# Weight decoding in a fused attention and squared-ReLU kernel: part of it moved to GpSimd, late weights two halves a piece, and three products held to the end

## The chip, the cores and the metric

The program runs on one NeuronCore of a Trainium2 chip. The metric is the device time of one execution in microseconds; for the kernel before the median of three runs is shown, and one execution was profiled.

## The reference, cut to what matters

```python
f = 1.0 / (1.0 + np.exp(-f_logit))              # B, H, S, D = 4, 8, 768, 48
for t in range(S):
    state = f[:, :, t, :, None] * state + np.einsum('bhd,bhe->bhde', k[:, :, t], v[:, :, t])
    y[:, :, t] = np.einsum('bhd,bhde->bhe', q[:, :, t], state)
x = y.transpose(0, 2, 1, 3).reshape(B * S, H * D)   # 3072 tokens x 384
h = x @ w_in                                        # 384 -> 2048
g = np.maximum(h, 0.0) ** 2
out = g @ w_out                                     # 2048 -> 384
```

A gated linear attention gives 3072 tokens of 384 numbers; two matrix products with a squared ReLU between them follow. The weights arrive as 64-bit floats.

## The kernel before, in words

**Tiling.** The 768 positions are cut into six blocks of 128; a block with its four batches is a tile of 512 columns. For every block the 2048 hidden units are taken in 16 *pieces* of 128. A piece `f` has three steps: `up` (L257, L277) makes `ph[f]` in PSUM from the block's `x` and the weights `w[f, 0]`; `square` (L283) and `rest` (L302) turn it into two f16 tiles, `gh` and `gl`, a high and a low part; `down` (L308) adds the products with `w[f, 1]` to three PSUM banks `po[0..2]`. Every product is made of three f16 matmuls (high by low, low by high, high by high), so `up` and `down` are nine 128x512 matmuls each. `ph` has two banks, three in the last block.

**Decoding a weight half.** A *half* is `w[f, i]`, 128x384 numbers, `i` = 0 for `w_in` and 1 for `w_out`. Its raw 64-bit words are loaded by a DMA from SP (`weights_load`, L453). `decode` (L141) then has four steps: ScalarE converts the upper 16 bits into `head` (L149); VectorE joins these with bits of the lower word into a float `wa` (L152); ScalarE makes the high f16 part (L162); VectorE makes the low part as a difference (L164). Four buffers of `head` and four of `wa` rotate.

**Attention units.** Each block has four *units*, a pair of heads each (the fourth collects left-over rows of the others). A unit has stages with one letter each (L708): gates `G` on ScalarE, `K` (two scans and products on VectorE, L503 and L511, and two small GpSimd operations, L507 and L510), `Q` (L517, L519, L522), `m` (DMAs that copy rows into `last_kq`, which the fourth unit reads; for units 0, 1, 4 and 5 they are issued by GpSimd, L530), `r` (ScalarE copies, L541), `D` and `S` (matmuls), `C` and `M` (VectorE), `Y` (matmuls), `H` and `X` (the halves of `x`), `g` and `h` (DMAs of the left-over rows, L704; `g` by GpSimd for the first two blocks).

**Order of the work.** All engines run in program order (`tc.manual_schedule`, L810). For blocks 0 and 1 that order is written out by hand in two strings, `FIRST` (L81) and `SECOND` (L86), one token a step. In them `A I c J` are the four decoding steps of `w[n, 0]`, `B O d P` those of `w[n, 1]`, `e n a w` those of a small fourth set of rows; `U`, `R`, `E`, `W` are `up`, `square`, `rest` and `down` of block 0. The strings decode the halves of pieces 0 to 7 and compute block 0's attention and pieces 0 to 7 and block 1's attention. After them come the runs of `order` (L822): block 1 with all 16 pieces, block 0 with pieces 8 to 15, then blocks 2 to 5. Steps are hung into a run with `hook(k, n, place, do)`: run `k`, piece `n`, place 0 (before `up`), 0.5 (after `square`), 0.7 (after `rest`) or 1 (at the piece's end). So the 16 halves of pieces 8 to 15 are decoded in the run of block 1, three in every two pieces, from piece 1 to piece 11 (L845 to L870); each is loaded four pieces ahead, behind a small VectorE memset that marks the time (L457). The units of later blocks are hung by `SLOTS` and `STAGE_AT`: for the first of them the gates and `K` fall at piece 6 of block 1, `Q` at piece 7, for the second `K` at piece 8, `Q` at piece 9.

**The end.** In a run `down` follows `up` by two pieces (`LAG`), in the last block by four (`LAST_LAG`). There the last four `down`s are done one `po` bank after the other (L325 to L334), each bank is scaled into `ob_last` (L332), and behind the first bank the *verdict* ends: the kernel checks that its numbers were in the range of f16 (`verdict`, L927) and reads a flag into a register on every engine (L905), on which a branch (L1092) depends that would compute everything another way. The outputs of the last block are written to DRAM behind that branch (L1098 to L1101). The first part of the verdict (four memsets, L937 to L940, two small copies, eight matmuls, L946 to L951, and reductions) hangs at the end of piece 7 of the last block (L901).

Of the kernel before, what the change touches and what calls it, by code (L numbers as in the profile page):

```python
# [12 lines left out]
F32 = mybir.dt.float32  # L13
# [10 lines left out]
P = 128  # L24
# [18 lines left out]
LARGE = 60000.0  # L43


X_SCALE, W_SCALE, G_SCALE = 2.0**16, 2.0**7, 2.0**18
ROOT = 2.0**-8
R_SCALE = G_SCALE**0.5 / (X_SCALE * W_SCALE)
O_SCALE = 1.0 / (G_SCALE * W_SCALE)
# [4 lines left out]
LAG = 2  # L54
LAST_LAG = 4
GBUF = 5
AHEAD = 4
LO = 8
SPLIT = 2
# [35 lines left out]
class Moe:  # L95


    def __init__(self, ctx, tc, const, sums, out):
        self.tc, self.nc, self.sums, self.out = tc, tc.nc, sums, out

        self.const, self.w, self.row, self.ps, self.turns, self.first = const, {}, {}, {}, 0, []
        self.xs, self.w4, self.third_bank, self.heads, self.half = [], None, None, 0, True

    def words(self, f, i):

# [32 lines left out]
    def upper(self, t, dt):  # L138
        return t.bitcast(dt).rearrange("p (n two) -> p n two", two=2)[:, :, 1]

    def decode(self, row, parts):  # L141


        nc = self.nc
        high, low = self.planes(row)
        rows, n = row.shape
        head = self.head[self.heads % HEADS][:rows, :n]
        self.heads += 1
        nc.scalar.copy(out=self.upper(head, F16), in_=high)  # L149
# [7 lines left out]
        yield from self.halves(parts(), a)  # L157

    def halves(self, w, a):
        nc = self.nc  # L160
        if self.half:
            nc.scalar.mul(out=w[:, 0], in_=a, mul=W_SCALE)  # L162
            yield
            nc.vector.scalar_tensor_tensor(  # L164
                out=w[:, 1], in0=a, scalar=W_SCALE, in1=w[:, 0], op0=ALU.mult, op1=ALU.subtract
            )
        else:
            nc.scalar.copy(out=w[:, 0], in_=a)
            yield
            nc.vector.tensor_tensor(out=w[:, 1], in0=a, in1=w[:, 0].bitcast(F32), op=ALU.subtract)  # L170
        yield

    def heads_in(self, pool):
# [109 lines left out]
    def square(self, f):  # L283

        nc, ph = self.nc, self.ph[f]
        dt = F16 if self.half else F32R
        gh, gl = (
            self.gp.tile([P, NT], dt, tag=t, name=f"{t}{self.blk}_{f}") for t in ("gh", "gl")
        )
        if self.half and f == 0:  # L290
            gh = self.pers.tile([P, NT], F16, name=f"first{self.blk}")
            self.first.append(gh)
        nc.scalar.activation(ph, ph, AF.Relu, scale=R_SCALE if self.half else 1.0)  # L293
        nc.scalar.activation(ph, ph, AF.Square)  # L294
        if self.half:
            n = 2 * NF + self.blk * NF + f
            nc.scalar.activation(gh, ph, AF.Copy, accum_out=self.sums[:, n : n + 1])  # L297
        else:
            nc.scalar.copy(out=gh, in_=ph)
        self.g[f] = gh, gl  # L300
# [17 lines left out]
    def run(self, hooks, obs=None, before=None, lag=LAG, ends=()):  # L318


        for n in range(len(self.fs) + lag):
            if before and not obs and n == len(self.fs) + lag - 1:
                return
            self.at = n
            if obs and n == len(self.fs):  # L325
                for e in range(NJ):
                    for f in self.fs[-lag:]:
                        self.down(f, (e,))
                    if e < len(ends):
                        ends[e]()  # L330
                    for _, cs in tails(e):
                        self.nc.vector.tensor_scalar(  # L332
                            out=obs[e][:, cs], in0=self.po[e][:, cs], scalar1=O_SCALE, scalar2=None, op0=ALU.mult
                        )  # L334
                return
            if n < len(self.fs):
                for hook in hooks.get((n, 0), ()):
                    hook()
                f = self.fs[n]
                self.up(f)  # L340
                self.square(f)
                for hook in hooks.get((n, 0.5), ()):
                    hook()
                self.rest(f)
                for hook in hooks.get((n, 0.7), ()):
                    hook()
            if before and n == 0:
                before()
                self.sums_of()
            if n >= lag:  # L350
                self.down(self.fs[n - lag])
            for hook in hooks.get((n, 1), ()):
                hook()
# [61 lines left out]
def fast_path(ctx, tc, moe, ident, low, fkqT, vN, w, w4, out):  # L415
# [338 lines left out]
    def step(t):  # L754
# [17 lines left out]
        elif nm == "j":  # L772
            nc.sync.dma_start(moe.fourth_words(), w4.bitcast(I16)[:, 1:])
        elif nm in "enaw":
            if nm == "e":
                decoding["fourth"] = moe.decode(moe.row4, moe.fourth_parts)
            next(decoding["fourth"])
        elif nm in "AIcJBOdP":
            i = "AIcJBOdP".index(nm) // 4
            if nm in "AB":  # L780
                decoding[n, i] = moe.decode(moe.row[n, i], lambda: moe.parts(n, i))
            next(decoding[n, i])
        elif nm in ("ua", "ub", "uc"):
# [26 lines left out]
    with tc.manual_schedule(engines={ET.PE, ET.SP, ET.DVE, ET.Activation, ET.Pool}):  # L810
# [14 lines left out]
        def hook(k, n, at, do):  # L825
            while n >= len(order[k][1]):
                k, n = k + 1, n - len(order[k][1])
            hooks[k].setdefault((max(n, 0), at), []).append(do)

        def third():  # L830
            early.close()
            moe.inputs(ctx)
            xs[2] = moe.new_x(2, 2)

# [2 lines left out]

        def advance(h):  # L840
            if h not in steps:
                steps[h] = moe.decode(moe.row[halves[h]], lambda: moe.parts(*halves[h]))
            next(steps[h], None)

        for n in range(1, NF - 1):  # L845
            few = range(3 * (n - 1) // 2, min(3 * n // 2, len(halves)))
            for h in few:
                if n < AHEAD:
                    weights_load(*halves[h])
                else:  # L850
                    hook(0, n - AHEAD, 0.5, lambda h=h: weights_load(*halves[h], mark=True))

            def before(few=few):
                for h, last in zip(few, (None, *few)):
                    for m in (h, h, last):
                        if m is not None:
                            advance(m)

            def after(few=few[:-1]):
                for h in few:  # L860
                    advance(h)

            def last(few=few):
                for h in few[-1:]:
                    advance(h)
                    advance(h)


            for place, do in zip((0, 0.5, 0.7) if n > 1 else (0.7, 0.7, 0.7), (before, after, last)):
                hook(0, n, place, do)  # L870
# [27 lines left out]
        for blk in range(NBLK):  # L898
            for j in range(NJ):
                hook(blk if blk > 1 else 1 - blk, TOP_AT + j, 1, lambda blk=blk, j=j: moe.size_of(blk, j, xs[blk][j]))  # L900
        hook(len(order) - 1, VERDICT_AT, 1, lambda: next(found))  # L901
        ends = (
            lambda: general.append(next(found)),
            lambda: None,
# [2 lines left out]
        for k, (blk, fs) in enumerate(order):  # L907
# [3 lines left out]
            if blk == NBLK - 1:  # L911

                moe.third_bank = ps_a
                obs = moe.third_of("ob_last")
                moe.run(hooks[k], obs, owed, LAST_LAG, ends)
                moe.third_bank = None
            else:
                moe.run(hooks[k], None, owed)
# [8 lines left out]
def verdict(nc, moe, low, ident, pool):  # L927
# [22 lines left out]
    nc.tensor.matmul(pt[0:1, 1, :DM], lhsT=sel[:, NBLK : NBLK + 1], rhs=v, start=True, stop=True)  # L950
    nc.tensor.matmul(  # L951
        pt[0:1, 1, DM : DM + 1], lhsT=tinies[:, 0:1], rhs=tinies[:, 1:2], start=True, stop=True
    )
    V.tensor_reduce(
        out=good[:, 0:1], in_=low.rearrange("p u n -> p (u n)"), axis=mybir.AxisListType.X, op=ALU.min
    )
    for n, x, least in (
        (1, pt[:NBLK, 0], ENOUGH), (2, pt[0:1, 1, :DM], ENOUGH), (3, pt[0:1, 1, DM : DM + 1], P * TINY**2 * 0.999)
# [19 lines left out]
def general_path(ctx, tc, moe, ident, fkqT, vN, w, out):  # L978

    nc = tc.nc  # L980
    moe.half = False
# [181 lines left out]
```

## Time and profile before

| | us |
|---|---|
| median of 3 runs | 468.21 (468.12 to 469.08) |
| the profiled execution's own time | 467.79 |
| its span in the trace | 466.1 |
| PE / PEld busy | 441.0 / 222.6 |
| DVE / ACT / POOL busy | 251.3 / 304.4 / 28.9 |

PE is TensorE's matmuls, PEld its weight loads, DVE VectorE, ACT ScalarE, POOL GpSimd, SP the engine that issues most DMAs. A busy time is the union of an engine's instructions. Times inside the trace count from the span's start. The granted TensorE clock was 0.997 of full speed over the span.

### The profile page before, as it was taken

The page shows a single profiled execution, that of the slowest core. Times are in us where ns is not written, and L with a number is a line of the kernel's source. Part 1 is how long each engine was busy: PE and PEld are TensorE (multiplying, and loading weights), DVE is VectorE, ACT ScalarE, POOL GpSimd, SP SyncE. Part 2 cuts the span into 40 slices and gives each one's busy share as a digit, 9 for nine tenths or more (in the row PEclk, how much of TensorE's full clock was granted, in tenths as well). Part 3 has the DMA queues.
Part 4 walks back from the last instruction along what each step waited for, and adds up shares of the span by engine and source line. Part 5 has one row for each costly group of instructions (what it writes and reads, how often), then busy time and mean ns, then how long its engine had stood idle before and what let it go on. Part 6 is the DMA issues. An engine that isn't in the chain of part 4 may idle for free.

```text
span 466.1 us, 11546 instructions
## 1 busy us (share of the span) xinstructions
PE 441.0 (95%) x4781; PEld 222.6 (48%) x4783; DVE 251.3 (54%) x467; ACT 304.4 (65%) x725; POOL 28.9 (6%) x66
## 2 busy tenths in 40 slices
PE   2889999998799999999999999999999999999994
PEld 2744554443354564455554455554455544444442
DVE  7999972668765636836444736534743321223122
ACT  4589975996765764676765877665966553853440
POOL 4411201001000000000000000000000000000000
PEclk9999999999999999999999999999999999999998
DMA  8798107373393334461133452233450000100002
GB/s 288 223 345 288 40 13 238 120 254 114 71 207 94 86 100 117 127 150 33 37 97 98 128 115 65 45 85 104 122 101 3 2 1 17 70 0 0 1 1 75
DMA packets 64749, 47.47 MB, mean 102 GB/s; under 512 B 46912, under 2 KB 50352, under 8 KB 64688
## 3 DMA queue, kind: packets, MB, share of 16 engines
q1 hardware_dynamic: 64096, 45.80, 34.7%
q0 software_dynamic: 448, 0.73, 0.7%
q8 instruction: 39, 0.64, 0.6%
q14 instruction: 22, 0.18, 0.1%
q10 hardware_dynamic: 144, 0.13, 0.1%
HBM read 35.22 MB, written 7.86 MB: 92 GB/s over the span
## 4 chain that ended last, share of the span: by engine, by line
PE 75%; ACT 8%; DVE 7%; DMA 5%; SPq 2%; issue 2%; POOL 0%; DVEq 0%
PE po L314 34%; PE ph L279 33%; DMA raw<-in_w_dram 2%; PE ds L615 2%; DMA fkq<-in_fkqT_dram 2%; PE ds L604 2%; ACT ph L294 2%; ACT gh L297 1%; ACT ph L293 1%; PE py L663 1%; ACT w L162 1%; DVE wa L152 1%; ACT head L149 1%; DVE fkq L519 1%; PE ph L675 1%
## 5 line engine op out<-in xcount | busy, mean ns | idle before, releaser
L279 PE MATMUL ph<-x,w 128*128 128x512 f16 x864 | 200.9, 379 | 5.0 <-DVE gl L304 4.3
L314 PE MATMUL po<-gh,w 128*128 128x512 f16 x540 | 160.6, 379 | 0.0
L304 DVE TENSOR_TENSOR gl<-ph,gh 128x512 f16<-128x512 f32 x90 | 62.1, 690 | 170.3 <-ACT gh L297 170.1
L279 PEld LDWEIGHTS <-w 128*128 128x128 f16 x870 | 84.5, 98 | 107.7 <-issue 7.6
L314 PEld LDWEIGHTS <-w 128*128 128x128 f16 x864 | 82.9, 98 | 98.8 <-issue 0.4
L293 ACT ACTIVATE ph<-ph 128x512 f32<-128x512 f32 x96 | 56.1, 584 | 103.1 <-PE ph L279 103.1
L314 PE MATMUL po<-gl,w 128*128 128x512 f16 x288 | 109.4, 380 | 0.1
L294 ACT ACTIVATE ph<-ph 128x512 f32<-128x512 f32 x96 | 55.9, 582 | 3.0
L297 ACT ACTIVATE gh<-ph 128x512 f16<-128x512 f32 x90 | 53.7, 597 | 2.8
L507 POOL TENSOR_SCALAR fkq<-fkq 128x8 f32<-128x8 f32 x18 | 12.7, 706 | 268.6 <-DVE fkq L503 177.6
L549 ACT COPY sx<-sp 48x208 f32<-48x208 f32 x44 | 16.0, 363 | 13.5 <-DVE sp L637 12.8
L503 DVE TENSOR_TENSOR_SCAN fkq<-fz,dr 128x520 f32<-128x520 f32 x18 | 22.2, 1233 | 1.9 <-ACT fz L498 1.9
L519 DVE TENSOR_TENSOR_SCAN fkq<-fz,dz 128x520 f32<-128x520 f32 x18 | 22.4, 1242 | 0.6
L162 ACT ACTIVATE w<-wa 128x384 f16<-128x384 f32 (+1 forms) x33 | 16.8, 515 | 7.9 <-DVE wa L152 7.4
L663 PE MATMUL py<-sc,vn 64*48 64x64 f32 (+1 forms) x384 | 20.8, 222 | 0.1
L149 ACT CAST head<-raw 128x384 f16<-128x384 bf16 (+1 forms) x33 | 19.2, 614 | 2.2 <-DMA raw<-in_w_dram 2.1
L663 PEld LDWEIGHTS py<-sc,vn 64*48 64x48 f32 (+1 forms) x384 | 16.4, 126 | 8.7 <-issue 8.7
L675 PE MATMUL py<-rx,sx 48*48 48x64 f32 x192 | 19.6, 216 | 0.1
L152 DVE SCALAR_TENSOR_TENSOR wa<-raw,head 128x384 int32<-128x384 int32 (+1 forms) x33 | 17.6, 547 | 2.9 <-ACT head L149 2.9
L164 DVE SCALAR_TENSOR_TENSOR w<-wa,w 128x384 f16<-128x384 f32 (+1 forms) x33 | 18.0, 548 | 1.6 <-ACT w L162 1.1
L297 ACT ACTIVATION_READ_ACCUMULATOR gh<-ph 128x1 f32 x90 | 17.5, 194 | 0.0
L663 PE MATMUL ph<-sc,vn 64*48 64x64 f32 (+1 forms) x256 | 16.6, 222 | 0.0
(125 smaller groups left out, 476.7 us busy)
## 6 DMA issues: line engine op xcount, KB each, us to landing
raw<-in_w_dram SPq DMA_DIRECT2D x32, 383.8 KB, 5.4
fkq<-in_fkqT_dram SPq DMA_DIRECT2D x15, 768.0 KB, 5.8
vn<-in_vN_dram SPq DMA_DIRECT2D x24, 192.0 KB, 4.4
steps<-fkq SPq DMA_DIRECT2D x48, 64.0 KB, 2.2
out_dram<-ob SPq DMA_DIRECT2D x12, 256.0 KB, 2.2
kn<-steps SPq DMA_DIRECT2D x12, 224.0 KB, 3.2
fkq<-in_fkqT_dram SPq DMA_DIRECT2D x9, 256.0 KB, 4.5
last_kq<-fkq SPq DMA_DIRECT2D x28, 64.5 KB, 3.2
```

Of the source, the lines that this page charges most:

```text
L149: nc.scalar.copy(out=self.upper(head, F16), in_=high)
L152: nc.vector.scalar_tensor_tensor(out=a.bitcast(I32), in0=low, scalar=13, in1=head.bitcast(I32), op0=ALU.logical_shift_right, op1=ALU.bitwi ...
L279: self.nc.tensor.matmul(self.ph[f], lhsT=w[:, i], rhs=x[:, j], start=first and n == 0, stop=last and n == 2)
L293: nc.scalar.activation(ph, ph, AF.Relu, scale=R_SCALE if self.half else 1.0)
L294: nc.scalar.activation(ph, ph, AF.Square)
L297: nc.scalar.activation(gh, ph, AF.Copy, accum_out=self.sums[:, n : n + 1])
L304: self.nc.vector.tensor_tensor(out=gl, in0=self.ph.pop(f), in1=gh if self.half else gh.bitcast(F32), op=ALU.subtract)
L314: self.nc.tensor.matmul(po[e], lhsT=l, rhs=r, start=f == fs[0] and i == 0, stop=f == fs[-1] and i == 2,)
L503: V.tensor_tensor_scan(out=rr[:, ::-1], data0=self.fz[:, NZ * CZ : 0 : -1], data1=dr[:, ::-1], initial=0.0, op0=ALU.mult, op1=ALU.add,)
L519: V.tensor_tensor_scan(out=pp, data0=self.fz[:, : NZ * CZ], data1=dz, initial=0.0, op0=ALU.mult, op1=ALU.add)
L663: nc.tensor.matmul(self.py[c][h * C : h * C + m, b * C : (b + 1) * C], lhsT=self.vn[rows, b, h * D : h * D + m], rhs=self.sc[rows, h, b], ...
L675: nc.tensor.matmul(self.py[c][h * C : h * C + m, b * C : (b + 1) * C], lhsT=s[rows, b * D : b * D + m], rhs=q[rows], start=False, stop=b = ...
```

## The change

`decode` gets an engine. With GpSimd as that engine, the high part (a copy) and the low part (a difference) are both made by it; the scale of the weights, now 2^8 instead of 2^7, is applied in the first step, where a factor of 2 on the f16 exponent bits does it. In the strings `FIRST` and `SECOND` every half but those in `SOON` and the small fourth set goes to GpSimd, in the run of block 1 all 16. There two halves are decoded in each of pieces 1 to 8, their first two steps at place 0 and GpSimd's two at place 0.5, and loaded four pieces ahead as before (six are loaded right away, four before). In the last block the `down`s of the loop end three pieces earlier, so that the last seven, not four, are done bank by bank; pieces 13 to 15 get `gh` and `gl` of their own in a pool `held`. The first part of the verdict is cut in two, at pieces 7 and 8.

```diff
+HOLD = 3
+SOON = ((0, 0), (1, 0), (0, 1))
...
-    def decode(self, row, parts):
+    def decode(self, row, parts, eng=None):
...
-        nc.scalar.copy(out=self.upper(head, F16), in_=high)
+        nc.scalar.mul(out=self.upper(head, F16), in_=high, mul=TOP_SCALE)
...
-        if self.half:
-            nc.scalar.mul(out=w[:, 0], in_=a, mul=W_SCALE)
-            yield
-            nc.vector.scalar_tensor_tensor(
-                out=w[:, 1], in0=a, scalar=W_SCALE, in1=w[:, 0], op0=ALU.mult, op1=ALU.subtract
-            )
+        if eng:
+            eng.tensor_copy(out=w[:, 0], in_=a)
         else:
             nc.scalar.copy(out=w[:, 0], in_=a)
...
+        yield
+        high = w[:, 0] if self.half else w[:, 0].bitcast(F32)
+        (eng or nc.vector).tensor_tensor(out=w[:, 1], in0=a, in1=high, op=ALU.subtract)
         yield
...
+        held = self.held and f in self.held[1]
+        pool, at = (self.held[0], f) if held else (self.gp, "")
...
-                    for f in self.fs[-lag:]:
+                    for f in self.fs[-lag - hold :]:
                         self.down(f, (e,))
...
-            if n >= lag:
+            if lag <= n < len(self.fs) - hold + (not hold) * lag:
                 self.down(self.fs[n - lag])
...
-                decoding[n, i] = moe.decode(moe.row[n, i], lambda: moe.parts(n, i))
+                decoding[n, i] = moe.decode(
+                    moe.row[n, i], lambda: moe.parts(n, i), None if (n, i) in SOON else G
+                )
...
-        for n in range(1, NF - 1):
-            few = range(3 * (n - 1) // 2, min(3 * n // 2, len(halves)))
-            for h in few:
+        for n in range(1, 1 + len(half[1])):
+            for h in (2 * n - 2, 2 * n - 1):
                 if n < AHEAD:
                     weights_load(*halves[h])
                 else:
                     hook(0, n - AHEAD, 0.5, lambda h=h: weights_load(*halves[h], mark=True))
...
+                for place, steps_now in (0 if n > 1 else 0.7, 2), (0.5 if n > 1 else 0.7, 2):
+                    for _ in range(steps_now):
+                        hook(0, n, place, lambda h=h: advance(h))
...
-        hook(len(order) - 1, VERDICT_AT, 1, lambda: next(found))
+        for n in range(2):
+            hook(len(order) - 1, VERDICT_AT + n, 1, lambda: next(found))
...
     nc.scalar.activation(v, moe.w[0, 1][:, 0], AF.Abs)
+    V.tensor_reduce(
+        out=good[:, 0:1], in_=low.rearrange("p u n -> p (u n)"), axis=mybir.AxisListType.X, op=ALU.min
+    )
+    yield
     pt = pool.tile([P, 2, 512], F32, tag="ab", name="totals")
```

## Rows read from the trace of the kernel before

**Rows 1.** Windows: stretch, length, busy us of PE, PEld, DVE, ACT, POOL

```profile
66.36:135.00 68.64, 64.48 (x472) 30.07 (x471) 43.48 (x87) 51.91 (x116) 3.65 (x8) 1.00 0.53 157
135.00:414.00 279.00, 278.67 (x3070) 140.06 (x3062) 135.55 (x237) 184.79 (x460) 9.39 (x20) 1.00 0.31 78
```

**Rows 2.** Windows of the hand-written lists and of block 1's run, columns as in Rows 1

```profile
31.00:73.45 42.45, 40.47 (x677) 22.10 (x670) 36.42 (x72) 36.21 (x84) 6.88 (x14) 1.00 0.39 128
73.45:125.00 51.55, 47.45 (x219) 21.04 (x217) 33.44 (x66) 40.44 (x90) 2.18 (x4) 1.00 0.53 172
```

**Rows 3.** Timeline, 419: the first matmul of the verdict

```profile
419.54 1.46 PE L946 MATMUL totals<-first,sel 128*6 128x512 f16 x6 [0.95 <-DVE tiny L940]
```

**Rows 4.** Waits in 66 to 140: us in total, times, longest

```profile
ACT w L162 <- DVE wa L152: 6.7, 5, 2.2
PE ph L279 <- DVE gl L304: 4.1, 4, 2.2
```

**Rows 5.** Timeline of ScalarE and TensorE, 109 to 125: start, us, idle before

```profile
109.21 0.52 ACT L162 ACTIVATE w<-wa 128x384 f16<-128x384 f32 x1 [2.20 <-DVE wa L152]
...
112.33 2.10 PE L279 MATMUL ph<-x,w 128*128 128x512 f16 x9 [1.37 <-DVE gl L304]
...
122.96 2.10 PE L279 MATMUL ph<-x,w 128*128 128x512 f16 x9 [2.19 <-DVE gl L304]
```

**Rows 6.** The page's costliest groups, three decoding steps: count, busy us, mean ns

```profile
L162 ACT ACTIVATE w<-wa 128x384 f16<-128x384 f32 (+1 forms) x33 | 16.8, 515 | 7.9 <-DVE wa L152 7.4
...
L149 ACT CAST head<-raw 128x384 f16<-128x384 bf16 (+1 forms) x33 | 19.2, 614 | 2.2 <-DMA raw<-in_w_dram 2.1
...
L164 DVE SCALAR_TENSOR_TENSOR w<-wa,w 128x384 f16<-128x384 f32 (+1 forms) x33 | 18.0, 548 | 1.6 <-ACT w L162 1.1
```

**Rows 7.** Groups of POOL by shape, whole span: count, busy us, mean ns

```profile
L507 POOL TENSOR_SCALAR fkq<-fkq 128x8 f32<-128x8 f32 x18 | 12.7, 706 | 268.6 <-DVE fkq L503 177.6 <-DMA vn<-in_vN_dram 59.8 <-DMA last_kn<-steps 26.5
L510 POOL TENSOR_SCALAR low<-fkq 128x8 f32<-128x8 f32 x18 | 4.8, 269 | 1.5
...
L439 POOL TENSOR_SCALAR_AFFINE_SELECT mask<-mask 64x64 f32<-64x64 f32 x2 | 0.5, 233 | 0.1
masks.py:199 POOL TENSOR_SCALAR_AFFINE_SELECT ident<-ident 128x128 f32<-128x128 f32 x1 | 0.3, 282 | 0.0
```

**Rows 8.** Timeline of DVE and POOL, 34 to 36: start, us

```profile
34.98 0.69 DVE L511 TENSOR_TENSOR fkq<-fkq 128x512 f32<-128x512 f32 x1
...
35.17 0.62 POOL L507 TENSOR_SCALAR fkq<-fkq 128x8 f32<-128x8 f32 x1
```

**Rows 9.** Groups of DVE in 31 to 73.45: count, busy us, mean ns

```profile
L152 DVE SCALAR_TENSOR_TENSOR wa<-raw,head 128x384 int32<-128x384 int32 x12 | 6.5, 551 | 1.4 <-ACT head L149 1.4
...
L519 DVE TENSOR_TENSOR_SCAN fkq<-fz,dz 128x520 f32<-128x520 f32 x2 | 2.5, 1242 | 0.1
...
L637 DVE TENSOR_TENSOR sp<-state,fkq 112x192 f32<-112x192 f32 x6 | 2.1, 354 | 0.1
```

**Rows 10.** POOL's copies into last_kq, ScalarE's reading of it, landing of POOL's copies

```profile
47.16 2.00 POOL L530 DMA_DIRECT2D last_kq<-fkq  x4
...
65.12 0.83 ACT L541 COPY rx<-last_kq 48x256 f32<-48x256 f32 x2
...
DMA to landing us min/median/max: 2.2/3.0/5.1
```

**Rows 11.** Timeline (the flag, the last DMA issues) and chain (the last matmuls)

```profile
455.57 0.14 DVE L974 CAST flag<-least 1x1 int32<-1x1 f32 x1
...
455.05 5.19 PE po L314 x24
...
460.03 1.34 SPq L1101 DMA_DIRECT2D out_dram<-ob_last  x3
```

**Rows 12.** DMA issues, 455 to 467 and whole span: count, KB each, us to landing

```profile
out_dram<-ob_last SPq DMA_DIRECT2D x1, 128.0 KB, 4.0
...
out_dram<-ob SPq DMA_DIRECT2D x12, 256.0 KB, 2.2
```

More of the change, by code (lines that the diff above doesn't have):

```diff
@@ L43 @@
 LARGE = 60000.0
-X_SCALE, W_SCALE, G_SCALE = 2.0**16, 2.0**7, 2.0**18
+X_SCALE, W_SCALE, G_SCALE = 2.0**16, 2.0**8, 2.0**18
+TOP_SCALE = W_SCALE ** (1 / 8)
 ROOT = 2.0**-8
@@ L102, in __init__ @@
         self.xs, self.w4, self.third_bank, self.heads, self.half = [], None, None, 0, True
+        self.held = None
     def words(self, f, i):
@@ L156, in decode, with halves @@
         yield
-        yield from self.halves(parts(), a)
-    def halves(self, w, a):
+        yield from self.halves(parts(), a, eng)
+    def halves(self, w, a, eng=None):
         nc = self.nc
-        if self.half:
-            nc.scalar.mul(out=w[:, 0], in_=a, mul=W_SCALE)
-            yield
-            nc.vector.scalar_tensor_tensor(
-                out=w[:, 1], in0=a, scalar=W_SCALE, in1=w[:, 0], op0=ALU.mult, op1=ALU.subtract
-            )
+        if eng:
+            eng.tensor_copy(out=w[:, 0], in_=a)
         else:
             nc.scalar.copy(out=w[:, 0], in_=a)
-            yield
-            nc.vector.tensor_tensor(out=w[:, 1], in0=a, in1=w[:, 0].bitcast(F32), op=ALU.subtract)
+        yield
+        high = w[:, 0] if self.half else w[:, 0].bitcast(F32)
+        (eng or nc.vector).tensor_tensor(out=w[:, 1], in0=a, in1=high, op=ALU.subtract)
         yield
@@ L286, in square @@
         dt = F16 if self.half else F32R
+        held = self.held and f in self.held[1]
+        pool, at = (self.held[0], f) if held else (self.gp, "")
         gh, gl = (
-            self.gp.tile([P, NT], dt, tag=t, name=f"{t}{self.blk}_{f}") for t in ("gh", "gl")
+            pool.tile([P, NT], dt, tag=f"{t}{at}", name=f"{t}{self.blk}_{f}") for t in ("gh", "gl")
         )
@@ L316, in down, with run @@
                 )
-    def run(self, hooks, obs=None, before=None, lag=LAG, ends=()):
+    def run(self, hooks, obs=None, before=None, lag=LAG, hold=0, ends=()):
         for n in range(len(self.fs) + lag):
@@ L828, in hook @@
             hooks[k].setdefault((max(n, 0), at), []).append(do)
+        held = []
         def third():
@@ L833, in third @@
             xs[2] = moe.new_x(2, 2)
+            held.append(ctx.enter_context(tc.tile_pool(name="held", bufs=1)))
         halves = [(f, i) for f in half[1] for i in range(2)]
@@ L841, in advance @@
             if h not in steps:
-                steps[h] = moe.decode(moe.row[halves[h]], lambda: moe.parts(*halves[h]))
+                steps[h] = moe.decode(moe.row[halves[h]], lambda: moe.parts(*halves[h]), G)
             next(steps[h], None)
-        for n in range(1, NF - 1):
-            few = range(3 * (n - 1) // 2, min(3 * n // 2, len(halves)))
-            for h in few:
+        for n in range(1, 1 + len(half[1])):
+            for h in (2 * n - 2, 2 * n - 1):
                 if n < AHEAD:
@@ L851, in fast_path @@
                     hook(0, n - AHEAD, 0.5, lambda h=h: weights_load(*halves[h], mark=True))
[L853 to L870, printed above, removed]
+                for place, steps_now in (0 if n > 1 else 0.7, 2), (0.5 if n > 1 else 0.7, 2):
+                    for _ in range(steps_now):
+                        hook(0, n, place, lambda h=h: advance(h))
         hook(0, 12, 0, third)
@@ L913, in fast_path @@
                 moe.third_bank = ps_a
+                moe.held = held[0], whole[-HOLD:]
                 obs = moe.third_of("ob_last")
-                moe.run(hooks[k], obs, owed, LAST_LAG, ends)
+                moe.run(hooks[k], obs, owed, LAST_LAG, HOLD, ends)
                 moe.third_bank = None
@@ L952, in verdict @@
         pt[0:1, 1, DM : DM + 1], lhsT=tinies[:, 0:1], rhs=tinies[:, 1:2], start=True, stop=True
-    )
-    V.tensor_reduce(
-        out=good[:, 0:1], in_=low.rearrange("p u n -> p (u n)"), axis=mybir.AxisListType.X, op=ALU.min
     )
@@ L980, in general_path @@
     nc = tc.nc
-    moe.half = False
+    moe.half, moe.held = False, None
     dram = ctx.enter_context(tc.tile_pool(name="dram", bufs=1, space=bass.MemoryType.DRAM))
```

## The prediction

> **What bounds the kernel now.** I read the windows first: for PE, busy time against the length of a stretch. From 135 to 414 us PE is busy for 278.67 of 279.00 us [rows 1]: there only fewer matmuls would help, and the change takes none away. What can be won lies where PE stands idle: 1.98 us from 31 to 73.45 (the end of the hand-written lists), 4.10 us from 73.45 to 125 (the run of block 1) [rows 2], 0.95 us at the verdict [rows 3], and the time behind the last matmul.
>
> Then the waits: in block 1's run PE waits 4.1 us in four places for `gl` of VectorE, and ScalarE 6.7 us for `wa` of VectorE [rows 4]. The timeline joins the two: at 109.21 the step L162 has held up ScalarE for 2.20 us, all behind it, the squares among it, come late, and PE waits 1.37 us at 112.33; the same shape comes back before 122.96 with 2.19 us [rows 5]. These are the pieces where the decoding and the later units' `K` and `Q` stand in one VectorE queue.
>
> **The change, part by part.** The sum is made against the profiled execution, 467.79 us with 466.1 in its span; the median is 0.42 us above it, and the result is given on the median.
>
> *The first step.* `mul` for a copy: L149 takes 614 ns, the `mul` of L162 515 ns on the same count [rows 6]. Between 0.1 us less and 0.1 more a half; I take no change, since the strided operands stay.
>
> *GpSimd's price.* No row shows a copy or a difference of 128x384 there. Two selects that read and write once take 233 ns for 64 columns and 282 ns for 128 [rows 7], so 0.184 us plus 0.766 ns a column: 0.48 us for 384. A difference reads twice: below 0.48 (nothing for the second operand), above 1.07 (three passes), and I take two passes, 0.184 + 2 x 0.294 = 0.77. A pair costs 1.25 us (0.96 to 1.55). The Trainium skill (GPSIMD Engine Reference, section 3.1) gives 4497 ns for a two-input add of 2048 columns; an estimate of 0.84 us for 384 by that page would make the pair 1.32 us and the sum below no other.
>
> *The lists, 31 to 73.45.* 13 halves of 16 move. ScalarE loses 12 x 0.515 = 6.2 us there (the thirteenth lies before 31), VectorE 13 x 0.548 = 7.1 us [rows 6]. VectorE was busy for 36.42 of 42.45 us [rows 2], so this looks like its relief. But the trace has a sign against it. L507 and L510 both work on 128x8 numbers, and one takes 706 ns where the other takes 269 [rows 7]; each L507 runs beside the L511 that follows its scan, and in the row shown it ends 0.12 us after it (35.79 and 35.67) [rows 8]. (Its columns lie apart, which may cost something; the end that follows L511's does not come from that.) So a GpSimd instruction that reads SBUF waits while VectorE reads two operands from SBUF. The Trainium skill (SBUF — State Buffer, Who interferes with whom) calls this an exclusive lock, which holds VectorE too when GpSimd came first. The rows agree with the first half; that VectorE waits no row shows.
>
> So I price both directions. VectorE's work with two SBUF operands in this stretch: `wa` 12 times, 6.5 us; four scans of 1.24, 5.0; L637 eight times 0.35, 2.8; five products of 0.69 (L511 and L522), 3.5 [rows 8, 9]: 17.8 of 42.45 us, or 42%. If 13 pairs of 1.25 (16.3 us) hold it up for that share of their length, it loses 6.8 us and wins 7.1: nothing either way. If they hold up nothing, PE's 1.98 us of idle time could go; if all of it, 16.3 - 7.1 - 6.03 (its idle time) = 3.2 us are lost. I take 0.3 us won, being nearest to the even case.
>
> *What queues up on GpSimd.* In its order `K`'s L507 now stands behind some high and low parts; the reader is `Q`, many tokens later, so I cost it at nothing. The DMAs of `g` come after `X` of the fourth unit, for which GpSimd waited anyway: nothing. The two DMAs of `m4` are another matter. They went out right behind `m5`'s, in the four that begin at 47.16 [rows 10]; now they stand behind `c6 J6`. From 47.2 GpSimd has six high and seven low parts and `m5` ahead of them: 6 x 0.48 + 7 x 0.77 + 1.0 = 9.3 us, and with waits for `wa` and for the lock I place their end near 60.3. Issued by 61.3, landed 2.2 to 5.1 us later (median 3.0), they arrive at 63.5 to 66.4, and ScalarE reads these rows at 65.12 [rows 10]. With the median just in time: nothing, and a rival.
>
> *Block 1's run.* Before, a piece with two halves gave ScalarE four steps and VectorE four; now ScalarE has two (the heads) and VectorE two (`wa`), and no squares stand behind a step that waits for VectorE. A piece has 18 matmuls, and 24 take 5.19 us in the chain [rows 11], so 3.9 us. ScalarE: two heads and four instructions of the square, some 3.1 us; VectorE two `wa` and `gl`, 1.8 us, and at most another 2 us for `K` or `Q`; GpSimd two pairs, 2.5 us (3.1 at the upper price). Each is under 3.9. VectorE: 33.44 us busy in 51.55 [rows 2] less 16 x 0.55 is 24.6, and 16 pairs held against it for the 42% add 8.4: still room. `gl` may come some 2 us later in a piece before `up` two pieces on needs its bank. The weights decoded at piece n are used at piece n + 7, so GpSimd's own lateness costs nothing. More halves are loaded early on SP, six at once: the last of them is read two pieces later. So of the 4.10 us I take 3.6: 0.5 us is left for the pieces where `K` and `Q` still meet the decoding. Ends: 0 and 4.1.
>
> *The verdict in two.* The 0.95 us was PE waiting for four memsets that stood behind `gl` on VectorE [rows 3]. A piece later they have long been made: 0.95 us won. The eight matmuls stay.
>
> *The last seven products.* The same matmuls in another order. Three `up`s follow each other; three banks and some 2.0 us of ScalarE for each square against 1.95 us of PE make no wait, and the last piece's products come after 18 matmuls of the earlier six. What moves is the flag. The first bank is done two banks before the end: before 2 x 12 matmuls, 5.2 us, now 2 x 21, 9.1 us, so 3.9 us earlier. Before, the flag stood at 455.71, and three output DMAs were issued at 460.03, just before PE's end at 460.24: two full banks of 256 KB and half of the last bank [rows 11]. They queued, and the last 128 KB took 4.0 us to land, where 256 KB mid-kernel take 2.2 [rows 12]. With the branch passed near 456, the first two banks are out while PE still works: 4.0 - 2.2 = 1.8 us won. Ends: 0 (the branch waits for something else) and 2.2.
>
> Sum: 0.3 + 3.6 + 0.95 + 1.8 = 6.65 us; 468.21 - 6.65 = 461.6.
>
> **The rivals.**
>
> *Late rows (m4).* GpSimd reaches `m4` later than I place it: at the upper price of a low part its seven cost 2.1 us more, the rows land near 66.4, ScalarE's copy stalls by 1.3 us and the matmuls of the fourth unit with it. For: the slack is under 2 us; against: VectorE and ScalarE are ahead by then, and so are GpSimd's inputs. Without the 0.3 and with 1.6 lost: 463.5.
>
> *Block 1's stalls stay.* VectorE's `K`, `Q` and two halves a piece make `gl` late again, now at pieces 7 to 9, the waits for L162 only give way to waits for the lock. For: both stalls stood at such pieces [rows 5]; against: ScalarE no longer stands behind `wa`. 468.21 - 0.95 - 1.8 - 0.3 = 465.2.
>
> *More than forecast.* The lists lose their idle time too: 1.98 + 4.1 + 0.95 + 1.8 = 8.8, so 459.4.
>
> *The shared port (slower).* Each GpSimd step holds up VectorE in full, as the lock would where VectorE always finds it taken. The lists lose 3.2 us, block 1's run wins nothing, and the verdict and the end give 2.75 back: 468.7; at 1.55 a pair the lists lose 7.0, which gives 472.5. It decides from a pair of (2.75 + 7.1 + 6.03)/13 = 1.22 us on, if nothing overlaps. For: my price is 1.25; against: over half of VectorE's time in the lists is not spent on two SBUF operands. This is what the rule of the SBUF page would do at its worst.
>
> *It doesn't do what it says.* The flag's register loads or the branch come no earlier and the freed engines leave PE where it was: only the 0.95 is won, 467.3.
>
> **How the numbers follow.** Forecast 0.50, with a range of its own from 460.3 to 463.0; late rows 0.16; stalls stay 0.14; more 0.07; shared port 0.08; not as said 0.05. A measurement here can tell 0.2%, 0.94 us, from no change: below 467.3 is faster. Four cases lie there for certain, 0.87; the last but one is slower in most of its span (0.07), the last stands on the edge. So 0.88 faster, 0.05 the same, 0.07 slower. The range runs from the "more" case, 459.4, past "stalls stay" to 466.2, and leaves out the last two cases and the outer ends of the others.
>
> **What would show it.** L162 and L164 with few instructions and POOL with 29 pairs at 0.5 and 0.8 us; wherever POOL and two-operand VectorE instructions meet, longer means of one of them (`wa` above 0.55 would show the lock). Windows of the lists with PE's idle time near 1.7 us and of block 1's run near 0.5; no wait for `tiny` at the verdict; the first two output DMAs issued some 4 us before PE's end, and 4 us, not 5.9, from the last matmul to the span's end. Wrong it would be if a low part takes over 1.1 us, if the copies from `last_kq` wait for a DMA, or if `gl` still ends PE's waits at pieces 7 to 10.

## The result, and the profile after

| | before | after |
|---|---|---|
| median, us | 468.16 (466.97 to 469.08) | 462.78 (461.94 to 463.25) |
| ratio, 95% interval | 1 | 0.9885 (0.9857 to 0.9912) |
| profiled execution: own time / span | 467.79 / 466.1 | 462.39 / 460.7 |
| DVE / ACT / POOL busy | 251.3 / 304.4 / 28.9 | 249.4 / 292.2 / 78.4 |

The kernel is 5.4 us faster; 461.6 was forecast. The windows of the kernel after are cut where block 1's first `up` starts, 73.28 (before: 73.45), so the first row answers to the first of [rows 2], the next two to the second of it and what followed, the last to the verdict [rows 3].

```profile
core 0: us, PE busy (x) PEld busy (x) DVE busy (x) ACT busy (x) POOL busy (x), PEclk, DMA share, GB/s
31.00:73.28 42.28, 39.90 (x682) 21.79 (x674) 34.65 (x60) 31.40 (x72) 26.27 (x38) 1.00 0.38 120
73.28:121.00 47.72, 47.30 (x236) 21.21 (x237) 34.58 (x49) 33.83 (x75) 30.52 (x37) 1.00 0.58 189
121.00:136.00 15.00, 15.00 (x245) 8.13 (x235) 9.26 (x19) 9.71 (x24) 0.95 (x2) 1.00 0.78 171
405.00:420.00 15.00, 15.00 (x72) 6.54 (x71) 3.95 (x12) 7.11 (x17) 0.00 (x0) 1.00 0.00 0
```

The reader is to see first minus second number of a row, TensorE's idle time: 2.38 us in the lists (before 1.98), 0.42 in block 1's run (4.10), none at the verdict (0.95). Two pieces of the chain of waits after say the same in times; the piece of before that answers to the first (`po`, behind block 1) stands below them, the one that answers to the second starts at 455.05 [rows 11].

```profile
376.64 2.05 PE po L317 x9
...
445.29 9.08 PE po L317 x42
```

```profile
381.49 2.05 PE po L314 x9
```

So the profiled pair differs by 0.17 us up to block 1's first `up` (73.45 to 73.28; the idle time in the lists grew by 0.40, so this comes from ahead of 31 us), by 4.68 from there to the `po` at 376.64, and by 1.02 from there to the last product (before 455.05 + 5.19 = 460.24, after 445.29 + 9.08 = 454.37). Behind the last product before needs 466.1 - 460.24 = 5.86 us and after 460.7 - 454.37 = 6.33: 0.47 is given back. Together 5.40, the difference of the own times.

The 4.68 us by TensorE's windows, from block 1's first `up` to that `po`, before and after:

```profile
73.45:381.49 308.04, 303.61 (x3292) 151.88 (x3291) 167.31 (x300) 212.34 (x518) 11.61 (x24) 1.00 0.39 102
73.28:376.64 303.36, 302.94 (x3292) 151.51 (x3291) 167.29 (x282) 205.21 (x502) 39.95 (x57) 1.00 0.39 104
```

4.01 us are idle time (4.43 less 0.42), and 0.67 lie in the busy time of the same 3292 matmuls.

The groups on the page after that answer to [rows 6, 9]:

```profile
L171 POOL TENSOR_TENSOR w<-wa,w 128x384 f16<-128x384 f32 x29 | 30.2, 1043 | 1.9
L156 DVE SCALAR_TENSOR_TENSOR wa<-raw,head 128x384 int32<-128x384 int32 (+1 forms) x33 | 24.5, 773 | 3.8 <-issue 2.0
...
L166 POOL CAST w<-wa 128x384 f16<-128x384 f32 x29 | 20.8, 719 | 17.1 <-DVE wa L156 16.8
```

`wa` takes 773 ns where it took 551: VectorE is held up. The timeline after shows it, and in both directions (start, length in us):

```profile
46.97 0.50 POOL L166 CAST w<-wa 128x384 f16<-128x384 f32 x1
47.44 0.93 POOL L171 TENSOR_TENSOR w<-wa,w 128x384 f16<-128x384 f32 x1
47.70 1.08 DVE L156 SCALAR_TENSOR_TENSOR wa<-raw,head 128x384 int32<-128x384 int32 x1
...
54.52 1.57 DVE L522 TENSOR_TENSOR_SCAN fkq<-fz,dz 128x520 f32<-128x520 f32 x1
55.07 1.72 POOL L171 TENSOR_TENSOR w<-wa,w 128x384 f16<-128x384 f32 x1
56.12 1.22 DVE L525 TENSOR_TENSOR fkq<-fkq 128x512 f32<-128x512 f32 x1
56.74 0.96 POOL L166 CAST w<-wa 128x384 f16<-128x384 f32 x1
```

At 47.70 `wa` stands until the difference is through (48.37) and ends 0.41 us later: 1.08 us. At 55.07 the difference came second: it stands behind the scan and takes 1.72 us, the product at 56.12 stands behind it, 1.22 us for one of 0.69, and the copy at 56.74 behind that, 0.96. Undisturbed, a copy takes 0.50 us and a difference 0.92.

### The profile page after: what moved, and what is told of

The parts are those of the page before. It is cut to its first block, busy times and chain, and to the rows that moved or that the text cites. A ratio compares the mean times of both kernels' runs of the same rounds, so it can differ in the third digit from the quotient of the medians.

```text
span 460.7 us, 11590 instructions
## 1 busy us (share of the span) xinstructions
PE 439.4 (95%) x4783; PEld 221.5 (48%) x4783; DVE 249.4 (54%) x436; ACT 292.2 (63%) x696; POOL 78.4 (17%) x124
## 4 chain that ended last, share of the span: by engine, by line
PE 82%; DVE 7%; DMA 5%; issue 2%; SPq 1%; ACT 1%; POOL 0%; DVEq 0%
PE po L317 37%; PE ph L280 36%; DMA raw<-in_w_dram 3%; PE ds L618 2%; DVE wa L156 2%; PE ds L607 2%; PE py L666 1%; DMA fkq<-in_fkqT_dram 1%; DVE fkq L522 1%; DVE fkq L506 1%; PE ph L678 1%; PE ph L666 1%; DMA vn<-in_vN_dram 1%; DVE gl L307 1%; SPq L494 1%
## 5 line engine op out<-in xcount | busy, mean ns | idle before, releaser
L171 POOL TENSOR_TENSOR w<-wa,w 128x384 f16<-128x384 f32 x29 | 30.2, 1043 | 1.9
L156 DVE SCALAR_TENSOR_TENSOR wa<-raw,head 128x384 int32<-128x384 int32 (+1 forms) x33 | 24.5, 773 | 3.8 <-issue 2.0
L166 POOL CAST w<-wa 128x384 f16<-128x384 f32 x29 | 20.8, 719 | 17.1 <-DVE wa L156 16.8
L153 ACT ACTIVATE head<-raw 128x384 f16<-128x384 bf16 (+1 forms) x33 | 18.9, 624 | 2.1 <-DMA raw<-in_w_dram 2.0
L645 DVE TENSOR_TENSOR state<-sp,ds 112x192 f32<-112x192 f32 x44 | 15.6, 354 | 2.3 <-PE ds L618 0.7
```

The lines of the kernel that those rows point to most:

```text
L156: nc.vector.scalar_tensor_tensor(out=a.bitcast(I32), in0=low, scalar=13, in1=head.bitcast(I32), op0=ALU.logical_shift_right, op1=ALU.bitwi ...
L171: (eng or nc.vector).tensor_tensor(out=w[:, 1], in0=a, in1=high, op=ALU.subtract)
```

## The experiments

Ratios are to the kernel before on the same chip; the kernel after has 0.9885 (0.9857 to 0.9912). Each edit is to the kernel after.

**Which part of the decoding pays?** First the lists' 13 halves back on ScalarE and VectorE:

```diff
-                    moe.row[n, i], lambda: moe.parts(n, i), None if (n, i) in SOON else G
+                    moe.row[n, i], lambda: moe.parts(n, i), None
```

> The changed kernel, but the 13 halves of the two hand-written lists are decoded by ScalarE and VectorE again; block 1's run keeps GpSimd. Theory (shared port, even): what VectorE and ScalarE are relieved of in the lists comes back as VectorE's waits for GpSimd, so the time is that of the changed kernel within 0.5 us and block 1's first up starts near 73.4 us. Rival 1 (the relief is real): 1 to 2 us slower. Rival 2 (the port costs more than the relief): up to 1 us faster.

462.42 us, ratio 0.9854 (0.9819 to 0.989): no slower, if anything faster. `wa` is back at 551 ns in the lists and stays at 923 ns in block 1's run; TensorE's idle time from 31 to block 1's first `up` (here 73.89) is 42.89 - 40.73 = 2.16 us, close to the 1.98 of before. The lists on GpSimd win nothing.

Then block 1's decoding on ScalarE and VectorE, two halves a piece as after:

```diff
-                steps[h] = moe.decode(moe.row[halves[h]], lambda: moe.parts(*halves[h]), G)
+                steps[h] = moe.decode(moe.row[halves[h]], lambda: moe.parts(*halves[h]))
```

> The changed kernel, but the 16 halves of block 1's run are decoded by ScalarE and VectorE, still two halves a piece in pieces 1 to 8; the lists keep GpSimd. Theory (the engines: ScalarE no longer stands behind wa): the waits of PE for gl come back, PE idles 3 to 5 us between 73 and 125, the time is 3 to 5 us longer. Rival (the schedule: two halves a piece, all of them before the second K and Q): the time stays within 1 us.

467.95 us, ratio 0.9977 (0.9958 to 0.9997): most of the gain is gone. The windows, then the waits from 66 to 140 (us in total, times, longest):

```profile
66.36:135.00 68.64, 65.39 (x456) 30.04 (x450) 42.55 (x83) 50.78 (x114) 5.66 (x10) 0.98 0.54 158
```

```profile
DVE w L171 <- ACT w L168: 8.8, 7, 1.7
...
PE ph L280 <- DVE gl L307: 3.2, 2, 2.6
```

TensorE idles 3.25 us where after it idles 0.42, and waits for `gl` again, as in [rows 4]. With this schedule it is VectorE that stands behind ScalarE (8.8 us), where before ScalarE stood behind `wa`.

**Engine or schedule?** The old schedule, three halves in two pieces, with GpSimd as the engine:

```diff
-        for n in range(1, 1 + len(half[1])):
-            for h in (2 * n - 2, 2 * n - 1):
+        for n in range(1, NF - 1):
+            few = range(3 * (n - 1) // 2, min(3 * n // 2, len(halves)))
+            for h in few:
...
```

> The decoding in the run of block 1 back to three halves in every two pieces (pieces 1 to 11, one step a hook), on GpSimd as in the kernel after. If the engine alone took the stalls away (ScalarE and VectorE lose a step each), TensorE idles no more in that run than after (0.5 us), time 462.3 to 463.3. If the bunched schedule with the GpSimd steps behind the square is needed too, part of the stalls is back: 1 to 3 us, time 463.8 to 465.8.

461.14 us, ratio 0.983 (0.9798 to 0.9862).

```profile
66.36:135.00 68.64, 68.64 (x613) 33.20 (x612) 40.78 (x77) 48.72 (x109) 33.34 (x46) 1.00 0.57 161
```

No idle time is left in the run, and VectorE is busy for 40.78 us, after for 46.53: spread out, `wa` meets GpSimd less often (625 ns, after 928). The engine alone takes the stalls away, and two halves a piece are not needed for it. Whether they cost something stays open, since the intervals overlap.

**What holds VectorE up?** GpSimd's steps replaced by memsets, which read nothing, so the kernel leaves the decoded values out and these weights are constants:

```diff
-            eng.tensor_copy(out=w[:, 0], in_=a)
+            eng.memset(w[:, 0], 1.0)
...
+            for _ in range(3):
+                eng.memset(w[:, 1], 0.0)
```

> GpSimd's two decoding steps are replaced by memsets, one of the high part and three of the low, so these weights are constants: as many GpSimd instructions that write the same tiles, but none that reads SBUF. If VectorE is held up by GpSimd's two reads of SBUF (or by a lock that only instructions with SBUF operands take), the mean of the step that joins the words falls from 0.77 back to 0.55 us and the scans from maxima of 1.9 to 1.24. If any GpSimd write holds it up, the mean stays above 0.65. TensorE's idle time is the same either way (0.5 us in the run of block 1), time 462 to 463.

459.06 us in one execution (span 457.4). The groups of the lists on VectorE and GpSimd (25 to 73 us), then the window from 31 to block 1's first `up`, here 71.19:

```profile
L156 DVE SCALAR_TENSOR_TENSOR wa<-raw,head 128x384 int32<-128x384 int32 x15 | 8.0, 553 | 2.2 <-ACT head L153 2.2
L173 POOL MEMSET w<- 128x384 f16 x39 | 16.2, 417 | 1.5
L166 POOL MEMSET w<- 128x384 f16 x13 | 5.4, 419 | 5.8 <-DVE wa L156 5.8
```

```profile
31.00:71.19 40.19, 39.59 (x689) 21.79 (x680) 30.81 (x60) 31.48 (x71) 24.80 (x61) 1.00 0.43 138
```

GpSimd works as long a half (4 x 0.42 = 1.67 us; in the lists after 0.67 + 1.02 = 1.69), yet `wa` is back at 553 ns. So it is GpSimd's reads that hold VectorE up. That TensorE's idle time would be the same either way was wrong: in the lists it falls to 0.60 us (after 2.38), and block 1 starts 2.1 us earlier; in block 1's run none of the 0.42 is left. Beside the 1.98 of before, GpSimd without its reads wins 1.4 us of idle time in the lists, and its reads take 1.8 back, in one execution of each kernel. TensorE's waits there after were for results of VectorE (0.64 for `state`, 0.48 for `sc`, 0.34 for `fkq`, 0.25 for `ys`) and 0.62 for ScalarE's `ph`, none for a weight; beside the memsets only the last is left, 0.50. The two largest of VectorE in the timeline after:

```profile
39.73 0.34 PE L666 MATMUL py<-sc,vn 64*64 64x64 f32 x8 [0.48 <-DVE sc L625]
...
51.29 0.34 PE L666 MATMUL py<-sc,vn 64*64 64x64 f32 x8 [0.64 <-DVE state L645]
```

(The high part's memset is also 0.08 us shorter than the copy, so a little of it may be that.)

**The hold, and the last landing.** No products held back:

```diff
-HOLD = 3
+HOLD = 0
...
-                moe.held = held[0], whole[-HOLD:]
+                moe.held = (held[0], whole[-HOLD:]) if HOLD else None
```

> The changed kernel with HOLD = 0: the last four products bank by bank as before, no tiles of their own. Theory (the last bank's DMA sets the end, whatever went out before it): the time is that of the changed kernel within 0.5 us, and from the last matmul to the span's end it is 5.9 us against 6.3. Rival (the early outputs do win 1.8 us and something else in the changed kernel took it away): 1.5 to 2 us slower.

463.75 us, ratio 0.9895 (0.9857 to 0.9933): not to be told from after. The last product ends where it does after (449.26 + 5.19 = 454.45). Next, the last bank sent as one transfer instead of two halves:

```diff
-    if e < NJ - 1:
-        return ((1, slice(0, NT)),)
-    return ((0, slice(0, NT // 2)), (1, slice(NT // 2, NT)))
+    return ((1, slice(0, NT)),)
```

> The changed kernel, but the last bank of the last block is scaled in one piece and sent by one DMA of SP, like the two banks before it. Theory (the 4.0 us to land belongs to the pair of half banks: rows of 1 KB, a second queue): it lands in 2.1 us like the others, and the time falls by 1.5 to 2 us. Rival (the last write of a program takes 4 us to be reported whatever its shape): the time stays within 0.5 us.

463.6 us, ratio 0.9889 (0.9851 to 0.9927). One whole transfer of 256 KB lands after 4.1 us, the halves after 4.0: neither their number nor the size of their rows sets it. The DMA view of the kernel after shows what does. Its packets by queue, from 455.5 to 457 and from 457 to 459 (q1 and q10 carry the outputs, q8 and q14 code):

```profile
q10 hardware_dynamic: 135, 0.12, 24.9%
q1 hardware_dynamic: 135, 0.12, 22.7%
q8 instruction: 1, 0.02, 7.3%
...
out_dram<-ob_last SPq DMA_DIRECT2D x1, 128.0 KB, 4.0
...
q10 hardware_dynamic: 9, 0.01, 2.6%
q14 instruction: 1, 0.01, 1.7%
q1 hardware_dynamic: 9, 0.01, 1.2%
```

135 of each transfer's 144 packets are through by 456.75; the last nine, a sixteenth, come from 457.5 on. In the first stretch a packet of code moves. It starts at 455.87, and its 7.3% of 16 engines' 1.5 us are 1.75 us: one DMA engine is taken until 457.6. Is it TensorE's code, loaded when it passes the branch behind its last product, or VectorE's, whose branch stands behind its last eviction? Two kernels delay one or the other:

```diff
+PAD = 8
...
+                    if e == NJ - 1:
+                        pad = self.ps["ps_h0"].tile([P, 512], F32, tag="ph", name="pad")
+                        for _ in range(PAD):
+                            self.nc.tensor.matmul(pad, lhsT=self.w[f, 1][:, 0, :P], rhs=self.first[0], start=True, stop=True)
```

> Eight more 128x512 matmuls on TensorE behind the last product (into a free bank, nothing reads them); otherwise the kernel after. In the kernel after, the last two 128 KB transfers are issued at 454.85 and 455.18 and land only after 4.0 us: nine of the 144 packets of each, one DMA engine's share, come at 457.5 to 458.75, after a code packet of queue q8 that starts at 455.75, 1.4 us after TensorE's last product, when it has passed the branch. Theory of TensorE's code load: with eight matmuls (1.7 us) more, that packet comes at about 457.5, when the data has moved; the two land after 2.0 to 2.6 us, and the time is 1.3 to 1.9 us shorter than the kernel after: 461.0 to 461.5. Rival, the load of VectorE (queue q14, it branches at 454.4 in either): landing stays at 4.0, time 462.8. Rival, a last transfer always takes so long: the same 4.0, time 462.8 or up to 1.7 more if TensorE's end counts.

461.78 us, ratio 0.9843 (0.9817 to 0.987; the interval of after begins at 0.9857, so the two still overlap a little). The last product ends at 446.45 + 9.06 = 455.51. The packets from 456.5 to 458, then from 458 to 459:

```profile
q10 hardware_dynamic: 144, 0.13, 26.5%
q1 hardware_dynamic: 144, 0.13, 24.1%
q14 instruction: 1, 0.01, 1.5%
...
out_dram<-ob_last SPq DMA_DIRECT2D x1, 128.0 KB, 2.1
...
q8 instruction: 1, 0.02, 6.1%
```

All 288 packets are through by 458, the q8 packet comes behind them, both halves land after 2.1 us, and 460.0 - 455.51 = 4.5 us remain behind the last product. VectorE's branch stands where it stood, behind the last eviction, and its load is not in the way: a packet of q14 moves among the data here too.

```diff
+                pad = self.gp.tile([P, NT], F16, tag="gl", name="pad")
+                for _ in range(2):
+                    self.nc.vector.tensor_tensor(out=pad, in0=obs[0], in1=obs[1], op=ALU.add)
```

> Two additions of 128x512 on VectorE (0.7 us each) behind its last eviction, otherwise the kernel after: VectorE's branch and its code load come 1.4 us later, TensorE's stay. Theory of TensorE's code load: the last two transfers still land after 4.0 us, the nine packets of each still come after the q8 packet; VectorE is ready at 458.7 instead of 457.3, before the landing at 459.2: time 462.8, the same. Rival, VectorE's load: landing 2.0 to 2.6, time about 462.0 (VectorE's own readiness, 458.7, then sets the end). Rival, a last transfer always takes so long: 4.0.

463.72 us, ratio 0.9871 (0.9835 to 0.9907): the same as after. Here q8 moves at 459.67, later against the last product than after; ScalarE's half is through (1.8 us), SP's loses its nine packets to it (3.8 us), and 6.2 us remain. So delaying TensorE's load frees the last transfers and delaying VectorE's doesn't. In time too the q8 packet goes with TensorE: it starts 0.7 us behind the end of TensorE's branch after (450.9 + 4.3 = 455.2, in the last lines of this text) and with the eight matmuls (457.5), while its distance to VectorE's branch is 1.5 and 2.6 us. In the kernel with the two additions it comes 1.6 us behind TensorE's branch (458.1), and what held it back there is not shown. What it hits depends on some tenths of a microsecond.

Is the hold worth something once the load is out of the way? The eight matmuls without the hold:

> Only the last four products bank by bank, as before the change, but with the eight matmuls behind the last product. Theory: what the seven held products are worth shows only when TensorE's code load no longer falls into the last transfers. Without the hold all four output transfers (768 KB) are issued within 1.3 us of each other at the end and need some 2.3 us of data, so the last lands 3.0 to 3.5 us after its issue, not 2.1, and from the last product to the end it is 5.3 to 5.8 us where the held and padded kernel has 4.5: 0.8 to 1.3 us longer, time 462.3 to 463.2. Rival, the hold is worth nothing either way: 4.5 us and 461.5.

462.51 us, ratio 0.9871 (0.9836 to 0.9906); 448.91 + 5.18 = 454.09 to 459.7, so 5.6 us behind the last product where the hold has 4.5, and 3.1 us for the last landing where it has 2.1. The hold is worth 1.1 us in these two profiles (without it the q8 packet, at 456.94, still meets the last packets); the ratios differ by 0.0028, 1.3 us, with intervals that overlap.

| profiled execution | last product | end of span | between | last landings |
|---|---|---|---|---|
| before | 460.24 | 466.1 | 5.9 | 4.0, 4.0 |
| after | 454.37 | 460.7 | 6.3 | 4.0, 4.0 |
| no hold | 454.45 | 461.7 | 7.2 | 4.7, 4.7 |
| no hold, eight matmuls | 454.09 | 459.7 | 5.6 | 2.7, 3.1 |
| hold, eight matmuls | 455.51 | 460.0 | 4.5 | 2.1, 2.1 |

**The verdict in one**, as before the change:

```diff
-        for n in range(2):
-            hook(len(order) - 1, VERDICT_AT + n, 1, lambda: next(found))
+        hook(len(order) - 1, VERDICT_AT, 1, lambda: (next(found), next(found)))
```

> The first part of the verdict back in one at the end of piece 7, otherwise the kernel after. TensorE waits again for the small copies on VectorE and ScalarE: 0.9 to 1.1 us of idle time between 405 and 420 (after: 0.00), all of it on the path. If another wait took its place or an earlier product covers it, under 0.3.

```profile
405.00:420.00 15.00, 14.05 (x67) 6.11 (x65) 4.46 (x16) 6.67 (x16) 0.00 (x0) 1.00 0.00 0
```

0.95 us of idle time is back, and the wait is for `tiny` again. (Its one time, 461.54 us, is below that of after: the landing took 2.6 us in it, since the q8 packet, at 455.88, began some half a microsecond ahead of the data.)

**Put together.** Three halves in two pieces and the eight matmuls; then the same with the lists' halves back as well:

> The two edits that were faster each, together: three halves in two pieces in the run of block 1 (on GpSimd), and eight more matmuls on TensorE behind the last product. If their gains lie in different places (0.4 us of idle TensorE between 66 and 135, 1.3 to 1.8 us behind the last product) they add: time 459.8 to 461.0, ratio to the kernel before 0.978 to 0.983. If the lower time of the spread schedule was only the scatter of the first 31 us, the time is that of the padded kernel alone: 461.3 to 462.0, ratio 0.984.

> As the one before it, and the lists' 13 halves back on ScalarE and VectorE. If GpSimd in the lists gives VectorE as much as it takes, the time is the same within 0.5 us. If what it holds up there (the step that joins the words 0.65 instead of 0.55, a scan each 0.1) is the larger, TensorE's idle time between 31 and 66 falls by 0.3 to 0.8 us and the time with it; if ScalarE's relief is the larger, it is 0.3 to 0.8 us longer.

461.77 us, ratio 0.9839 (0.9816 to 0.9862): the gains did not add in the median. With the lists back 459.8 us, ratio 0.98 (0.9776 to 0.9823): the fastest of all that decode their weights, 1.97 us under the other, whose interval it only touches, and clear of the kernel after. The timeline of the first of the two shows where GpSimd hurts the lists:

```profile
47.92 1.09 POOL L538 DMA_DIRECT2D last_kq<-fkq  x2
48.32 1.85 DVE L645 TENSOR_TENSOR sp<-state,fkq 112x192 f32<-112x192 f32 x1
49.03 0.93 POOL L172 TENSOR_TENSOR w<-wa,w 128x384 f16<-128x384 f32 x1
...
52.27 0.34 PE L671 MATMUL py<-sc,vn 64*64 64x64 f32 x8 [2.00 <-DVE state L650]
```

A product of 0.35 us [rows 9] stands while GpSimd issues two DMAs, loses the race against the difference at 49.03 as well, and takes 1.85 us; TensorE then waits 2.00 us for `state`. In the kernel after the same instruction takes 1.07 us and TensorE waits 0.6. The issues by themselves hold nothing up: before, four of them run from 47.16 to 49.16 [rows 10], with no decoding step behind them, and VectorE's two-operand steps beside them take their usual time:

```profile
48.35 0.55 DVE L152 SCALAR_TENSOR_TENSOR wa<-raw,head 128x384 int32<-128x384 int32 x1
48.82 0.35 DVE L637 TENSOR_TENSOR sp<-state,fkq 112x192 f32<-112x192 f32 x1
```

What held the product from 48.32 to 49.03 stays open; the difference next in GpSimd's queue is the only decoding step near it, but no run separates that. Of ten profiled kernels with the lists' differences on GpSimd, four have the 2.0 (three halves in two pieces, the single last transfer, VectorE's two additions, and this one), six have 0.6: two outcomes of one race.

## Why the prediction was right, and where its sum was off

The forecast case held, 1.2 us from its number; its terms did not all. That the sum came so near is in part luck: one term was 1.1 us too small, another 2.3 us too large.

*The lists, 0.3:* 0.17 in the profiled pair, and nothing or a loss over the runs. The even case came about, and the evidence of [rows 7, 8] was the right evidence; the other direction, which no row showed, is there: VectorE is held up as well. The balance behind it was off. By the mean times of its steps in the lists it lost some 4.1 us (six products before `state`, 0.35 to 0.64, 1.7; twelve `wa`, 0.55 to 0.67, 1.4; other products and scans 1.0), where 6.8 was forecast, and 7.1 went away. 4.1 against 7.1 still gave TensorE nothing: the prediction weighed VectorE's time in sum, and what counted were the results that TensorE waits for next, `state` and `sc` (0.64 and 0.48 us, with no such wait before). The Trainium skill (SBUF — State Buffer, Who interferes with whom) says that VectorE instructions with two SBUF inputs contend with GpSimd instructions that read SBUF and not with those that only write; the trace agrees, in both directions (1.08 for 0.55 us, 1.72 for 0.92) and with the memsets. `gl`, which reads one operand from PSUM, kept its 0.69 us.

*GpSimd's price, 1.25 a pair:* 0.50 + 0.92 = 1.42 undisturbed. The high part was right, the low part 0.77 is 0.92 (inside its ends; the 0.84 estimated from the Trainium skill's GPSIMD Engine Reference, section 3.1, is nearer). 1.42 is over the 1.22 from which the slower rival was to decide, and it did not come, because it needed every step to be held up in full.

*Block 1's run, 3.6:* 4.68, above the upper end of 4.1. The reason stands (engine back on ScalarE and VectorE: the stalls are back). The half microsecond left for pieces with `K` and `Q` is there (0.42, of it 0.31 in one wait for `gl` at 110.66), so 4.10 - 0.42 = 3.68 is the term as it was meant. It was mis-sized by what it did not count: 0.33 us of idle time behind 125, and 0.67 us in TensorE's busy time. For a matmul in front of a stall shows 0.38 us, one that the next follows at once 0.22, so each stall cost some 0.16 us more than its idle time.

*The verdict, 0.95:* 1.02, and 0.95 when undone.

*The last seven products, 1.8:* this step failed; the profiled pair loses 0.47. The flag came early as worked out: SP issued the first two outputs at 450.18, 4.2 us before the last product's end, and they landed after 2.1 us. But "they queued, and the last 128 KB took 4.0 us to land" put all of the 4.0 down to the queue. After, the last two still took 4.0 with nothing ahead of them; TensorE's code load held a sixteenth of their packets. Before, a q8 packet started at 461.77, among the data as well, and 41 of the four transfers' 576 packets still came from 463.25 on:

```profile
q1 hardware_dynamic: 25, 0.03, 5.0%
q10 hardware_dynamic: 16, 0.01, 2.4%
```

With the eight matmuls on both sides the queue shows nearly by itself: landings of 2.7 and 3.1 us without the hold, 2.1 with it, and 5.6 - 4.5 = 1.1 us for the step, within its ends and below the 1.8.

*Late rows:* the two DMAs of `m4` began at 60.08, near the place given them, and ScalarE read the rows at 63.87 without a wait. *Stalls stay* and *not as said* did not happen; *more than forecast* did in block 1's run alone.

## What to carry to other kernels

An engine that looks idle may share a port: ask how many operands of the neighbour's instructions come from SBUF, and give it work where that neighbour has slack (block 1's run), not where its results are waited for next (the lists). Spread out, such work met its neighbour less often (`wa` 0.63 for 0.93 us), though no run shows a gain in time clear of the noise for that. When a transfer at the end lands late, count its packets by time and see which other queue moved, before its size or its queue is blamed; here a branch behind an engine's last instruction loaded code just when the last output moved.

## What the runs showed of the hardware

- GpSimd's reads and VectorE's two-operand instructions from SBUF exclude each other: `wa` 0.55 us alone, 0.93 on average in block 1's run beside 16 pairs, and 0.55 beside memsets of the same length.
- GpSimd's DMA issues alone do not count among these: before, `wa` took 0.55 us and a product 0.35 beside them. In the kernel with three halves in two pieces and the eight matmuls, where a difference comes next, a product stood from 48.32 on; why is open.
- A packet of TensorE's code of 0.02 MB took 1.75 us at the end, and nine of 144 packets of each of the last two outputs came 1 to 2 us behind the others, and with them the landing, 4.0 instead of 2.1 us.
- SP's first instruction behind the branch came 2.5 us after it (446.9 and 449.4), and three packets of q14 moved in between. The Trainium skill (Runtime: NRT & Kernel Launch, Instruction fetch mechanics) says that a taken branch to code not yet loaded forces a DMA fetch; the trace agrees, and the run with the eight matmuls adds that TensorE's fetch is in the way of data.

```profile
L1086 SPq EVENT_SEMAPHORE  x8: 17/17/17, 449.4 to 450.0; - x8
...
L1086 SPq COMPARE_BRANCH  x1: 50/50/50, 446.9 to 446.9; - x1
...
L1086 PEldq COMPARE_BRANCH  x1: 4282/4282/4282, 450.9 to 450.9; - x1
```
